# Attention in front of two feed-forward layers: transposing probabilities by halves of the queries

## The chip, the cores and the metric

The kernel runs on one core of one Trainium2 chip. The metric is the device time of one execution in microseconds (us). The core has a matmul engine (TensorE, PE in the profile; its weight loads are shown apart as PEld), VectorE (DVE), ScalarE (ACT), GpSimd (POOL) and SyncE (SP), which issues most transfers. Each engine works through its own queue in order, and semaphores tie the queues together. TensorE writes only to PSUM, an accumulation memory of eight banks, from which DVE and ACT copy results out.

## The reference

Attention over two batches of eight heads, 768 positions, head size 64, each query seeing the last 128 positions and the first four ("sinks"), and two feed-forward layers of width 512 to 2048 to 512 on the 1536 tokens:

```python
keep = is_sink | in_window
scores = np.where(keep, scale * np.matmul(q, k.transpose(0, 1, 3, 2)), -1000000000.0)
a = np.exp(scores - np.max(scores, axis=-1, keepdims=True))
a = a / (np.sum(a, axis=-1, keepdims=True) + 1e-09)
x = np.matmul(a, v).transpose(0, 2, 1, 3).reshape(B * S, H * D)
h = np.maximum(x @ w_in, 0.0)
x = h * h @ w_out
h = x @ moe2_w_in
out = (h * np.tanh(softplus(h))) @ moe2_w_out
```

## The kernel before

The program has two stages. The first, up to about 106 us, is attention; the second is the two layers, whose matmuls (L620 and L636) fill the rest of the span.

Attention goes by blocks of 128 queries, 12 in all (tile number t), each with the 128 positions before it, its own 128 and a strip of 16 sink columns: at most 272 columns of scores. Heads are taken two at a time; a block has four such *pairs* (j = 0 to 3), and there are 48 pairs. The loop at L541 walks over *slots* n, one per pair; in each slot several pairs are at different steps. `at[d]` is the pair n + d, and `last` holds the d whose pair is the last of its block. The order in which the code emits work is the order of every engine's queue.

- `emit_s` (L350): scores of a pair on PE. Six matmuls, three for each of the two heads; queries and keys are split into a high and a low part (`qh`, `ql`, `kh`, `kl`). Each matmul has 64 rows (the head size), and the two heads lie in the upper and the lower 64 rows of the array.
- `emit_max` (L363): adds the mask and takes the maximum, on DVE, once per head.
- `emit_exp` (L372): the exponential and its sum, on ACT, once per head, into `pr`.
- `emit_rs` (L384): adds up the sums and takes their reciprocal for two pairs, on DVE. `emit_norm` (L395): multiplies the probabilities of a pair by it, on POOL.
- `emit_t` (L401): transposes the probabilities of a pair on PE, 128x128 each, against the identity; two heads and up to two blocks of keys make four. They go into one PSUM bank (`pt`). `evac_t` (L411) copies the bank to `pts`, on DVE where j is 0 (`EV = (0,)`, L181) and on ACT otherwise.
- `emit_av` (L420): the products with v, with `pts` as the moving operand; each fills 64 of the array's 128 columns.
- `emit_sink` (L435, POOL), `emit_sink_t` (L443, PE), `evac_sink` (L452, DVE) and `emit_sink_mm` (L458, PE): gathers, transposes, copies and multiplies the sink columns of a whole block.
- `emit_x` and `split_x` (L474, L480): the finished block out of its one PSUM bank, high part on ACT (`xh`), low part on DVE (`xl`).
- `prep` (L294) and `place_prep` (L317): transposes q or k of a later block on PE (L302, four of 128x128), copies the high part on ACT (L314), subtracts for the low part on DVE (L320).

The steady state has a rhythm of two slots. In an even slot PE has the scores of pair n + 4, `prep`, the transposes of pairs n - 1 and n, and behind the last pair of a block its sink transpose. In an odd slot it has scores and the products with v of pairs n - 3 and n - 2, and the sink products. The scores have four PSUM banks, two pairs' worth; `pt` and the transposes of q and k share three; the products with v have one. Four blocks of the first layer's weights are converted on the side (L129 to L166) in some of the slots.

Of the kernel before, what the change touches and what calls it, by code (L numbers as in the profile page):

```python
# [9 lines left out]
F32 = mybir.dt.float32  # L10
# [7 lines left out]
P = 128  # L18
# [10 lines left out]
def kernel(  # L29
# [13 lines left out]
    nc = tc.nc  # L43
    B, H, S, D = q.shape
# [4 lines left out]
    NPAIR = H // 2  # L49
# [131 lines left out]
    EV = (0,)  # L181
# [146 lines left out]
    def geom(i):  # L328

        if i == 0:  # L330
            return kpos(0), P, mask0, None, 0, None
        if i == 1:
            return kpos(0), 2 * P, mask1, 0, P, None
        if i % 2 == 0:
            return kpos(i - 1), WIN, mask_e, 0, P + SK, P
        return kpos(i - 1) - SK, WIN, mask_o, SK, SK + P, 0
# [5 lines left out]
    pair_no = {p: m for m, p in enumerate(pairs)}  # L342

    def sum_at(b, i, j):
        g, s = divmod(pair_no[b, i, j] + 1, 2)
        return sums[g % len(sums)], s
    st = {}
    pr = {}
# [49 lines left out]
        x = pr[b, i][:, 2 * j : 2 * j + 2, 0:w]  # L398
        nc.gpsimd.tensor_tensor(out=x, in0=x, in1=rs.to_broadcast([P, 2, w]), op=ALU.mult)  # L399

    def emit_t(b, i, j):  # L401
        _, _, _, op, oc, _ = geom(i)
        pt = ps_p.tile([P, 2, 2, P], F32, tag="pt", name="pt")
        for e in range(2):
            h = 2 * j + e
            if op is not None:
                nc.tensor.transpose(pt[:, 0, e, :], pr[b, i][:, h, op : op + P], ident)  # L407
            nc.tensor.transpose(pt[:, 1, e, :], pr[b, i][:, h, oc : oc + P], ident)  # L408
        st["pt", b, i, j] = pt

    def evac_t(b, i, j):  # L411
        pt = st.pop(("pt", b, i, j))
        pts = apool.tile([P, 2, 2, P], F32, tag="pts", name="pts", bufs=3)
        c = slice(0 if i else 1, 2)
        (nc.vector.tensor_copy if j in EV else nc.scalar.copy)(pts[:, c], pt[:, c])
        st["pts", b, i, j] = pts

    av = {}

    def emit_av(b, i, j):  # L420
        _, _, _, op, _, os_ = geom(i)
        if j == 0:
            av[b, i] = ps_a.tile([P, NPAIR, P], F32, tag="av", name="av")
        pts = st.pop(("pts", b, i, j))
        blocks = [(1, i)] if op is None else [(0, i - 1), (1, i)]
        for m, (c, kb) in enumerate(blocks):
            for e in range(2):
                nc.tensor.matmul(  # L428
                    av[b, i][e * D : (e + 1) * D, j, :], lhsT=vn[b, kb][:, 2 * j + e, :],
                    rhs=pts[:, c, e, :], start=(j == 0 and m == 0),  # L430
                    stop=(j == NPAIR - 1 and m == len(blocks) - 1 and os_ is None),
                    skip_group_check=True,
                )
# [60 lines left out]
    with tc.manual_schedule():  # L494
        load_limits()
        nc.scalar.preload_act_table_set("natural_log_exp_and_others")
        load_tile(0, "qk", halves=2)
        load_tile(1, "qk")
        load_tile(2, "kq")
        load_tile(0, "v")  # L500
        load_tile(3, "kq")
        positions()
        load_tile(1, "v")
        load_vsink(0)
        load_tile(2, "v")
        load_tile(3, "v")
        warm = apool.tile([P, P], F32, name="warm")
        nc.vector.memset(warm, 0.0)
        nc.vector.memset(one, 1.0)
        nc.gpsimd.memset(two, 2.0)  # L510
        for x in sums:
            nc.vector.memset(x, 1e-9)
        idle = ps_a.tile([P, P + 2], F32, tag="av", name="idle")

        def keep_warm(times):
            for _ in range(times):
                nc.tensor.matmul(idle[:, 0:P], lhsT=warm, rhs=warm, start=True, stop=True)  # L517

        keep_warm(WARM[0])
        limits(idle[:, P : P + 2])  # L520
        first_mask()
        prep(0, "q", 0)
        place_prep()
        keep_warm(WARM[1])
        prep(0, "k", 0)
        place_prep()
        keep_warm(WARM[2])
        emit_s(*pairs[0])
        emit_max(*pairs[0], 0)
        emit_max(*pairs[0], 1)  # L530
        prep(0, "q", 1)
        place_prep()
        prep(0, "k", 1)
        place_prep()
        emit_s(*pairs[1])
        emit_max(*pairs[1], 0)
        emit_max(*pairs[1], 1)
        second_mask()
        window_masks()
        emit_exp(*pairs[0])  # L540
        for n in range(-3, NPR + 4):  # L541
            at = {d: pairs[n + d] for d in range(-3, 5) if 0 <= n + d < NPR}
            last = {d for d in at if at[d][2] == NPAIR - 1}
            t, j = divmod(n, NPAIR)
            if 4 in at and n > -3:
                emit_s(*at[4])
            if 3 in at and n > -3:
                emit_exp(*at[3])
            if n % 2 == 0:
                group = [at[d] for d in (1, 2) if d in at]  # L550
                if group:
                    emit_rs(group)
                for p in group:
                    emit_norm(*p)
                    if p[2] == NPAIR - 1:
                        emit_sink(*p[:2])
            if -3 in last:
                emit_x(*at[-3][:2])
            if 4 in at and n > -3:
                emit_max(*at[4], 0)  # L560
                emit_max(*at[4], 1)
            split_x()


            if n % 2 == 0:
                if n >= 0:
                    prep(t + 2, "kq"[j // 2])
                for d in (-1, 0):
                    if d in at:
                        emit_t(*at[d])  # L570
                if -1 in last:
                    emit_sink_t(*at[-1][:2], st["s", *at[4]][0] if 4 in at else None)
            else:
                for d in (-3, -2):
                    if d in at:
                        emit_av(*at[d])
                if -2 in last:
                    emit_sink_mm(*at[-2][:2])
            if -1 in at:
                evac_t(*at[-1])  # L580
            if n in (-3, -2):
                prep(1, "qk"[n + 3])
            place_prep()
            evac_sink()
            if n >= 0 and j == NPAIR - 1:
                load_tile(t + 4, "q")
                load_tile(t + 4, "k")
                load_tile(t + 4, "v")
            if n == -1 or (n >= 0 and t < len(tiles) - 1 and (t % NB, j) == (NB - 1, 2)):
                sink_keys()  # L590
            if n < 0:
                keep_warm(WARM[3])
            if n == 1:
                fast_flag()
                load_vsink(1)
            if n in (5, 13):
                spread_vsink(n // 8)
            for m, x in enumerate(blocks):
                step = CONV_STEPS.get(n - CONV_AT[0] - CONV_AT[1] * m)
                if step:  # L600
                    getattr(x, step)()
# [416 lines left out]
```

## Time and profile before

| | |
|---|---|
| median of 3 runs | 636.59 us (635.65 to 636.65) |
| span of the profiled execution | 633.9 us |
| total of the profiled execution | not listed; the median of the runs lies 2.7 us over the span |
| PE busy | 623.8 us, 98% of the span |
| DVE, ACT, POOL busy | 461.6, 364.1, 71.1 us |
| attention stage | the first 106 us |

The span runs from the first to the last instruction of one profiled execution. A busy PE is not a PE at its peak, as matmuls are pipelined and one's end overlaps the next one's start. So the rows below go by starts: from the start of one group of instructions to the start of the next.

### The profile page before, as it was taken

Reading aid. Unit: us, or ns where it says so; the run is one execution under the profiler, and the core shown is the slowest. Engines: PE = TensorE matmul, PEld = TensorE weight load, DVE = VectorE, ACT = ScalarE, POOL = GpSimd, SP = SyncE. Lnnn points to the kernel's source line nnn. Section 1 sums busy time; section 2 is a strip of 40 time slices with the busy share of each in tenths; the row PEclk is TensorE's granted clock in tenths of the full one; section 3 lists DMA queues with packets and bytes.
Section 4 is the critical chain, followed back from the end, with each engine's and each line's share of the span. In section 5 each row is a group of like instructions: output and inputs, shape, how many; then the busy total and the mean of one; then the engine's idle time right before and its main releaser. Section 6 shows DMA issues by size and latency. Waiting matters only on the chain.

```text
span 633.9 us, 9250 instructions
## 1 busy us (share of the span) xinstructions
PE 623.8 (98%) x3382; PEld 515.3 (81%) x3382; DVE 461.6 (73%) x967; ACT 364.1 (57%) x745; POOL 71.1 (11%) x97
## 2 busy tenths in 40 slices
PE   8999999999999999999999999999999999999995
PEld 7878877888888888888888888888888888888884
DVE  6988983999842111138988879999888888888883
ACT  5988985777744333347777655555454444454441
POOL 4786773000000000000000000000000000000000
PEclk9999999999999999999999999999999999999998
DMA  9644630666630000005566600000010000010001
GB/s 205 152 121 101 165 125 8 199 203 199 197 100 0 2 0 1 0 1 187 185 195 198 199 0 1 0 2 1 1 66 1 1 1 1 22 46 0 2 0 71
DMA packets 60968, 46.87 MB, mean 74 GB/s; under 512 B 38900, under 2 KB 55284, under 8 KB 60916
## 3 DMA queue, kind: packets, MB, share of 16 engines
q1 hardware_dynamic: 60768, 45.95, 24.5%
q8 instruction: 28, 0.46, 0.3%
q10 hardware_dynamic: 148, 0.26, 0.1%
q14 instruction: 24, 0.20, 0.1%
HBM read 43.06 MB, written 3.15 MB: 73 GB/s over the span
## 4 chain that ended last, share of the span: by engine, by line
PE 96%; DVE 2%; ACT 1%; issue 0%; DVEq 0%
PE h L620 41%; PE o L636 41%; PE s L356 4%; PE av L428 3%; PE tr L302 2%; PE pt L408 1%; PE pt L407 1%; PE idle L517 1%; PE av L464 1%; DVE s L367 1%; ACT pr L379 0%; DVE cv_a L147 0%; DVE cv_r L137 0%; ACT kh L314 0%; DVE cv_r L141 0%
## 5 line engine op out<-in xcount | busy, mean ns | idle before, releaser
L620 PE MATMUL h<-xl,wih 128*128 128x512 f32 x384 | 103.2, 390 | 0.0
L620 PE MATMUL h<-xh,wil 128*128 128x512 f32 x384 | 103.0, 390 | 0.0
L620 PE MATMUL h<-xh,wih 128*128 128x512 f32 x384 | 102.6, 389 | 0.0
L687 DVE TENSOR_TENSOR gl<-h,gh 128x512 fp32r<-128x512 f32 x48 | 33.2, 691 | 92.7 <-ACT gh L683 92.7
L620 PEld LDWEIGHTS h<-xl,wih 128*128 128x128 f32 x384 | 72.0, 188 | 15.2 <-issue 0.3
L620 PEld LDWEIGHTS h<-xh,wih 128*128 128x128 f32 x384 | 72.1, 188 | 15.0
L620 PEld LDWEIGHTS h<-xh,wil 128*128 128x128 f32 x384 | 71.9, 188 | 15.0 <-issue 0.2
L703 ACT ACTIVATE e<-t,small 128x512 f32<-128x512 f32 x48 | 34.8, 725 | 70.4 <-DVE t L699 70.4
L636 PE MATMUL o<-gh,wol 128*128 128x512 f32 x192 | 74.7, 389 | 0.0
L636 PE MATMUL o<-gl,woh 128*128 128x512 f32 x192 | 74.7, 389 | 0.0
L636 PE MATMUL o<-gh,woh 128*128 128x512 f32 x192 | 74.7, 389 | 0.0
L681 ACT ACTIVATE h<-h 128x512 f32<-128x512 f32 x48 | 27.9, 582 | 77.4 <-PE h L620 77.3
L636 PE MATMUL o<-wol,gh 128*128 128x512 f32 x176 | 68.5, 389 | 0.0
L636 PE MATMUL o<-woh,gl 128*128 128x512 f32 x176 | 68.5, 389 | 0.0
L636 PE MATMUL o<-woh,gh 128*128 128x512 f32 x176 | 68.5, 389 | 0.0
L719 ACT CAST gh<-t 128x512 fp32r<-128x512 f32 x44 | 27.4, 623 | 46.4 <-PE o L636 43.0
L399 POOL TENSOR_TENSOR pr<-pr,rs 128x544 f32<-128x544 f32 (+2 forms) x48 | 48.4, 1022 | 23.0 <-DVE rs L391 15.2
L147 DVE SCALAR_TENSOR_TENSOR cv_a<-cv_a,cv_r 128x512 int32<-128x512 int32 x64 | 44.5, 695 | 6.5 <-ACT h L681 0.5
L379 ACT ACTIVATE pr<-s,nm 128x272 f32<-128x272 f32 (+2 forms) x96 | 44.4, 477 | 5.1 <-DVE nm L367 2.6
L724 DVE TENSOR_TENSOR gl<-t,gh 128x512 fp32r<-128x512 f32 x44 | 30.3, 690 | 19.8 <-ACT gh L719 19.8
L636 PEld LDWEIGHTS o<-gl,woh 128*128 128x128 f32 x192 | 36.1, 188 | 7.6
L636 PEld LDWEIGHTS o<-gh,wol 128*128 128x128 f32 x192 | 36.0, 188 | 7.5
(119 smaller groups left out, 1100.6 us busy)
## 6 DMA issues: line engine op xcount, KB each, us to landing
raw<-in_moe_w_in_dram SPq DMA_DIRECT2D x32, 512.0 KB, 3.9
raw<-in_moe_w_out_dram SPq DMA_DIRECT2D x32, 512.0 KB, 4.2
vn<-in_v_dram SPq DMA_DIRECT2D x12, 256.0 KB, 2.9
qn<-in_q_dram SPq DMA_DIRECT2D x11, 256.0 KB, 4.3
kn<-in_k_dram SPq DMA_DIRECT2D x11, 256.0 KB, 4.2
out_dram<-ob SPq DMA_DIRECT2D x4, 512.0 KB, 3.6
out_dram<-o SPq DMA_DIRECT2D x3, 256.0 KB
qn<-in_q_dram SPq DMA_DIRECT2D x2, 128.0 KB, 2.9
```

Source lines behind the costliest of these rows:

```text
L147: nc.vector.scalar_tensor_tensor(out=ai, in0=ai, scalar=3, in1=self.r, op0=ALU.logical_shift_left, op1=ALU.bitwise_or)
L356: nc.tensor.matmul(banks[e][:, 0:w], lhsT=x[b, i][r, j, :], rhs=y[r, j, c0 : c0 + w], start=(m == 0), stop=(m == 2),)
L379: nc.scalar.activation(out=pr[b, i][:, 2 * j + e, 0:w], in_=banks[e][:, 0:w], func=AF.Exp, bias=nm[:, e : e + 1], scale=-1.0, accum_out=sm ...
L399: nc.gpsimd.tensor_tensor(out=x, in0=x, in1=rs.to_broadcast([P, 2, w]), op=ALU.mult)
L428: nc.tensor.matmul(av[b, i][e * D : (e + 1) * D, j, :], lhsT=vn[b, kb][:, 2 * j + e, :], rhs=pts[:, c, e, :], start=(j == 0 and m == 0), s ...
L620: nc.tensor.matmul(ph, lhsT=w[a][:, d, :], rhs=x[:, d, :], start=(m == 0 and d == 0), stop=(m == 2 and d == NDC - 1),)
L636: nc.tensor.matmul(acc[sp][t], lhsT=a, rhs=x, start=(fb == 0 and m == 0), stop=(fb == NFB - 1 and m == 2),)
L681: nc.scalar.activation(out=ph, in_=ph, func=AF.Relu)
L687: nc.vector.tensor_tensor(out=gl, in0=hp.pop(n), in1=f32(gh), op=ALU.subtract)
L703: nc.scalar.activation(out=e, in_=t, func=AF.Ln, bias=two)
L719: nc.scalar.copy(g_tiles(n)[0], et[n][1])
L724: nc.vector.tensor_tensor(out=gl, in0=t, in1=f32(gh), op=ALU.subtract)
```

## The change

The transposes of the probabilities are cut by queries: the upper and the lower 64 rows (queries) of a block are transposed apart, each against a 64x64 corner of the identity, into one of two PSUM banks, so that 64 rows of the array take part in each. Two pairs are transposed together, and each of the two banks holds one half of the queries of both pairs. Each bank is copied out in a slot of its own, into alternate runs of 64 columns of `pts`.

The order in the slots changes with it. Transposes of q and k and the sink transpose move from even slots to odd ones, ahead of the products with v. The transposes of an even slot are those of pairs n and n + 1 in place of n - 1 and n; sums and normalisation are those of n + 2 and n + 3 in place of n + 1 and n + 2, and they are emitted behind the maxima of pair n + 4.

```diff
     def sum_at(b, i, j):
-        g, s = divmod(pair_no[b, i, j] + 1, 2)
+        g, s = divmod(pair_no[b, i, j], 2)
...
+    def emit_t(group):
+        banks = [ps_p.tile([P, 2, 2, 2, P // 2], F32, tag="pt", name="pt") for _ in range(2)]
+        for s, (b, i, j) in enumerate(group):
+            _, _, _, op, oc, _ = geom(i)
+            for e in range(2):
+                for c, o in enumerate((op, oc)):
+                    if o is None:
+                        continue
+                    for r in range(2):
+                        rows = slice(r * D, (r + 1) * D)
+                        nc.tensor.transpose(
+                            banks[r][:, s, c, e, :], pr[b, i][rows, 2 * j + e, o : o + P], ident[rows, rows]
+                        )
+        pts = apool.tile([P, 2, 2, 2, P], F32, tag="pts", name="pts", bufs=2)
+        for s, p in enumerate(group):
+            st["pts", p] = pts[:, s]
+        st["evac"] = [(group, banks[r], pts[..., r * D : (r + 1) * D], r) for r in range(2)]
+
+    def evac_t(eng=None):
+        if not st.get("evac"):
+            return
+        group, x, y, r = st["evac"].pop(0)
+        copy = nc.vector.tensor_copy if r and pair_no[group[0]] % 4 in EV else nc.scalar.copy
+        c0 = [0 if i else 1 for _, i, _ in group]
+        if len(set(c0)) == 1:
+            copy(y[:, : len(group), c0[0] :], x[:, : len(group), c0[0] :])
+        else:
+            for s, c in enumerate(c0):
+                copy(y[:, s, c:], x[:, s, c:])
...
+            if -3 in last:
+                emit_x(*at[-3][:2])
+            if 4 in at and n > -3:
+                emit_max(*at[4], 0)
+                emit_max(*at[4], 1)
             if n % 2 == 0:
-                group = [at[d] for d in (1, 2) if d in at]
+                group = [at[d] for d in (2, 3) if d in at]
                 if group:
                     emit_rs(group)
                 for p in group:
                     emit_norm(*p)
                     if p[2] == NPAIR - 1:
                         emit_sink(*p[:2])
-            if -3 in last:
-                emit_x(*at[-3][:2])
-            if 4 in at and n > -3:
-                emit_max(*at[4], 0)
-                emit_max(*at[4], 1)
             split_x()
             if n % 2 == 0:
-                if n >= 0:
-                    prep(t + 2, "kq"[j // 2])
-                for d in (-1, 0):
-                    if d in at:
-                        emit_t(*at[d])
-                if -1 in last:
-                    emit_sink_t(*at[-1][:2], st["s", *at[4]][0] if 4 in at else None)
+                if 0 in at:
+                    emit_t([at[0], at[1]])
             else:
+                if n >= -1:
+                    prep(*((t + 3, "k") if j == NPAIR - 1 else (t + 2, "q")))
+                if 0 in last:
+                    emit_sink_t(*at[0][:2], st["s", *at[4]][0] if 4 in at else None)
                 for d in (-3, -2):
                     if d in at:
                         emit_av(*at[d])
                 if -2 in last:
                     emit_sink_mm(*at[-2][:2])
-            if -1 in at:
-                evac_t(*at[-1])
+            evac_t()
```

## Rows read from the trace of the kernel before

**Rows 1.** The page: the chain that ended last, shares by engine.
```profile
PE 96%; DVE 2%; ACT 1%; issue 0%; DVEq 0%
```
**Rows 2.** Windows of 10 us: PE, PEld, DVE, ACT, POOL busy (instructions); granted clock.
```profile
20.00:30.00 10.00, 10.00 (x109) 8.26 (x110) 9.23 (x37) 9.77 (x33) 7.09 (x8) 1.00 0.39 103
...
sum 70.00, PE 68.92 PEld 57.14 DVE 62.31 ACT 62.59 POOL 51.41; mean PE 9.85 PEld 8.16 DVE 8.90 ACT 8.94 POOL 7.34
```
**Rows 3.** Weight loads in order of time, 70 to 74 us: start, us, what.
```profile
70.14 0.19 PEld L356 LDWEIGHTS s<-kh,qh 64*128 64x128 f32 x2 [0.17 <-ACT qh L314]
...
70.71 0.85 PEld L428 LDWEIGHTS av<-pts,vn 128*64 128x64 f32 x16
71.74 0.19 PEld L356 LDWEIGHTS s<-kh,qh 64*128 64x128 f32 x2 [0.17 <-issue]
71.84 0.19 PEld L356 LDWEIGHTS s<-kh,ql 64*128 64x128 f32 x2
71.97 0.19 PEld L356 LDWEIGHTS s<-kl,qh 64*128 64x128 f32 x2
72.31 0.42 PEld L302 LDWEIGHTS tr<-ident,kn 128*128 128x128 f32 x4
72.70 0.14 PEld L407 LDWEIGHTS pt<-ident,pr 128*128 128x128 f32 x1
...
73.46 0.14 PEld L408 LDWEIGHTS pt<-ident,pr 128*128 128x128 f32 x1
73.77 0.19 PEld L356 LDWEIGHTS s<-kh,qh 64*128 64x128 f32 x2 [0.17 <-ACT pr L379]
```
**Rows 4.** Weight loads from 92.2 us, a group of transposes with no tr ahead.
```profile
92.87 0.14 PEld L407 LDWEIGHTS pt<-ident,pr 128*128 128x128 f32 x1
92.93 0.14 PEld L408 LDWEIGHTS pt<-ident,pr 128*128 128x128 f32 x1
```
**Rows 5.** The chain that ended last, in order of time: start us, us, what.
```profile
83.47 0.87 PE av L464 x16
```
**Rows 6.** Groups of ACT's instructions, 20 to 90 us: count, busy us, mean ns.
```profile
L415 ACT COPY pts<-pt 128x512 f32<-128x512 f32 x24 | 14.5, 602 | 0.0
...
L314 ACT CAST kh<-tr 128x512 fp32r<-128x512 f32 x8 | 4.7, 586 | 1.2 <-PE tr L302 0.9
```
**Rows 7.** The page: transfers, count, KB each, median us to landing.
```profile
kn<-in_k_dram SPq DMA_DIRECT2D x11, 256.0 KB, 4.2
```
**Rows 8.** DVE in order of time from 73.4 us.
```profile
73.49 0.15 DVE L390 TENSOR_REDUCE rs<-sum 128x4 f32<-128x8 f32 x1
...
73.77 0.42 DVE L367 CUSTOM_DVE_ANT_0 s<-s,mask_o 128x272 f32<-128x272 f32 x1
...
74.51 0.69 DVE L320 TENSOR_TENSOR kl<-tr,kh 128x512 fp32r<-128x512 f32 x1
```
**Rows 9.** POOL in order of time from 73.4 us.
```profile
74.00 2.15 POOL L399 TENSOR_TENSOR pr<-pr,rs 128x544 f32<-128x544 f32 x2 [2.56 <-DVE rs L391]
```
**Rows 10.** Who waited for whom, 14 to 104 us: total us, times, longest.
```profile
PEld s L356 <- ACT pr L379: 2.5, 11, 0.6
...
PEld pt L407 <- POOL pr L399: 0.2, 1, 0.2
```
**Rows 11.** Groups of PE's instructions, 20 to 90 us.
```profile
L408 PE MATMUL pt<-ident,pr 128*128 128x128 f32 x72 | 16.0, 273 | 0.0
L407 PE MATMUL pt<-ident,pr 128*128 128x128 f32 x64 | 15.0, 274 | 0.0
```
**Rows 12.** Windows, 90 to 105.8 us, columns as in the earlier windows.
```profile
90.00:95.00 5.00, 4.60 (x60) 3.77 (x61) 5.00 (x17) 4.09 (x15) 3.89 (x5) 1.00 0.54 180
...
100.00:105.80 5.80, 5.80 (x66) 4.46 (x65) 0.98 (x2) 2.18 (x4) 0.70 (x2) 1.00 0.01 4
```
**Rows 13.** PE in order of time, 75 to 76.2 us, scores released apart.
```profile
75.69 0.51 PE L356 MATMUL s<-kh,ql 64*128 64x272 f32 x2
75.92 0.41 PE L356 MATMUL s<-kl,qh 64*128 64x272 f32 x2
```

More of the change, by code (lines that the diff above doesn't have):

```diff
@@ L399, in emit_norm @@
         nc.gpsimd.tensor_tensor(out=x, in0=x, in1=rs.to_broadcast([P, 2, w]), op=ALU.mult)
[L401 to L416, printed above, removed]
+    def emit_t(group):
[26 more added lines that the diff above has]
+                copy(y[:, s, c:], x[:, s, c:])
     av = {}
@@ L423, in emit_av @@
             av[b, i] = ps_a.tile([P, NPAIR, P], F32, tag="av", name="av")
-        pts = st.pop(("pts", b, i, j))
+        pts = st.pop(("pts", (b, i, j)))
         blocks = [(1, i)] if op is None else [(0, i - 1), (1, i)]
```

## The prediction

> **What bounds the kernel now.** I began with the page's chain of work that ended last: 96% of it lies on TensorE (PE) [rows 1]. Most of that is the two feed-forward layers, which the change doesn't touch; it touches the attention stage, up to about 106 us, so the question is what bounds that stage. The table of windows from 20 to 90 us answers only half: PE is busy 68.9 of 70 us, but VectorE (DVE) 62.3 and ScalarE (ACT) 62.6, or 89% each, and in its fullest window of 10 us ACT reaches 9.77 [rows 2]. The granted clock there is 1.00, so none of this is the clock. PE is first, two engines stand close behind it. A cheaper PE therefore can't shorten these 70 us by more than the distance to the second and third engine, and that distance is the main term of my sum.
>
> The timeline of PE's weight loads shows one steady period of two slots [rows 3]. A score group (L356) starts at 70.14, the products with v (L428) at 70.71, the next scores at 71.74, the transposes of keys (L302) at 72.31, those of the probabilities (L407/L408) at 72.70, the next scores at 73.77: 0.57 + 1.03 + 0.57 + 0.39 + 1.07 = 3.63 us. Inside a group the loads follow each other evenly: a pair of score matmuls (two heads, in the two row halves of the array) every 0.11 to 0.13 us, a transpose every 0.11 us. Between groups of a different layout there is more: 0.34 us from the last score pair to the first transpose, 0.31 us from the last transpose to the next scores. So a change of layout costs about 0.2 us, and the period has four (64x128 scores to 128x128 transposes, back, to 128x64 products, back). From tr to pt, both 128x128, there is none.
>
> **PE's part of the change.** (1) *Layouts.* The probabilities' transposes become 64x128, as the scores are, so in an even slot scores, transposes and the next scores share one layout; the transposes of q and k go to the odd slot between scores and products. The changes left are scores to tr, tr to av, av to scores: three in place of four, 0.2 us saved per period. No row shows 64x128 transposes beside 64x128 scores; the nearest, tr to pt, shows no gap within a layout, and I take none.
>
> (2) *The transposes.* Eight of 128x128, 8 x 0.11 = 0.87 us, become sixteen of 64x128 in eight pairs, one pair into two PSUM banks. What does a pair cost? Two things pace a transpose, loading 128 columns of weights and streaming the identity's columns. They come apart at the first one of a group that stands alone: the second load begins 0.06 us after the first, and only from then on every 0.11 us [rows 4]. So the load takes 0.06 and the streaming of 128 columns 0.11. A half streams 64 columns, 0.055 us, so the load sets the pace: 0.06 us a pair if the two halves run side by side, 8 x 0.06 = 0.47 us. That they do is what the score pairs show: two loads and two matmuls of 64 rows every 0.12 us [rows 3]. Bounds: 0.47 us for the group below; above, no overlap and a load as long as today's whole transpose, 16 x 0.11 = 1.75 us. I take 0.47, plus 0.05 before the next scores for their own first load. The period on PE becomes 0.36 + 0.47 + 0.05 + 0.57 + 0.59 + 1.03 = 3.07 us (0.59 is tr with its change of layout): 0.56 us less.
>
> The Trainium skill, page "TensorE: Matmul & The Clock Gate", section "LDWEIGHTS (loading the stationary operand)", puts a weight load at columns/1.2 ns however few rows it has. By it 128 columns take 107 ns, a pair of halves costs as much as a whole transpose, the group stays at 0.87 us, and only the layout change is saved; that is the second rival. The row with 0.06 us speaks against it, for this kind of load.
>
> (3) *Sinks.* The sink's transpose (L449) now follows tr in the odd slot, same layout, 0.11 us as before. Its products (L464) stay behind those with v [rows 5].
>
> **The other engines.** Their work is the same in amount. Evacuations: still two of 512 elements per two pairs, still a quarter on DVE; they now write runs of 64 of a wider tile. The nearest row for such writes: the copy into kh, runs of 128 of a wide tile, takes 586 ns, the one into contiguous pts 602 [rows 6]. I take no change; the lower end is the same, as no row shows a gain from shorter runs, and the upper one a tenth more for each of the 24 copies on ACT in these 70 us, 24 x 0.06 = 1.4 us. The loads of q, k and v are issued as before. k of block t+3 is now prepared at slot 4t+3 in place of 4t+4, which leaves four slots, two periods or 7.3 us, from issue; the page gives 4.2 us from issue to landing [rows 7], so I count nothing; if that cover were gone, the lost slot would cost up to half a period, 1.8 us, per block of queries.
>
> The *order* changes. Normalisation of a pair (POOL, L399) was emitted one or two slots behind its exponential; for the later pair of each two it is now in the same slot, and DVE's reduction and reciprocal (L390, L391) stand behind both maxima of that slot. They must wait for ACT's two exponentials, and behind them on DVE wait xl, the low half of q or k and the next maxima. The way from scores to transposes, from rows: scores some 0.45 us (of the 0.57 above), two maxima 0.74 (74.51 - 73.77), reduction and reciprocal 0.28 (73.77 - 73.49), then 0.2 to POOL, two normalisations 2.15 [rows 8, 9]: with 0.3 for the hand-overs 4.1 us from the start of the scores of an even slot to the second half of the next even slot's transposes. PE gets there after one period plus 0.6 us, 3.7 us in a period without sink products and 4.6 with the 0.87 us of L464. So in every second period some 0.1 to 0.4 us are missing even if DVE is never late. Between 14 and 104 us of the kernel before, PE waited for POOL once, 0.2 us [rows 10].
>
> **The sum.** From 20 to 90 us lie 136 whole transposes of probabilities [rows 11], 17 full groups, so PE alone would allow 17 x 0.56 = 9.5 us. DVE and ACT don't: 62.6 us of ACT work fit in no less. Between today's mean of 89% and the best window's 97.7% I take 95%: 62.6/0.95 = 65.9 us, **-4.1 us** (ends: 91%, -1.2; 97.7%, -5.9). From 90 to 95 us DVE is busy throughout; from there to 105.8, when no scores are left, DVE is mostly idle, ACT half, and PE is full, with the first products of the feed-forward layer between those of attention [rows 12]. There PE's work counts in full: the last five pairs have 20 transposes, which at 0.05 us less each give 1.0 us, and one group with two layout changes goes, 0.4, against two sink transposes that now stand alone, +0.4: **-1.0** (-0.4 to -1.6). Late normalisations and a second bank that comes free after the first: **+0.7** (the 0.1 to 0.4 us above in the half of 17 periods without sink products give 0.9 to 3.4 us; other waits on PE hide part, so the ends are 0 and 3, and I take a value near the low one). Start-up, where inputs are awaited: 0. Together -4.4 us. The feed-forward stage follows on a full PE, so the gain reaches the end. The profiled execution has a span of 633.9 us; its own total is not listed, and the three runs have a median of 636.59, so 2.7 us lie around the span, which I carry unchanged: 629.5 us of span, **632.2 us**; this case by itself 629 to 635.3.
>
> **Rivals.** *First, the gain is swallowed (about 636.3, within 0.2%).* ACT and DVE are each idle 11%, but in pieces that the hand-overs need; scores already wait for ACT's exponentials in 11 places [rows 10], and PE with less to do only waits longer. For it: 97.7% in one window already [rows 2]. Against: PE's idle time is the smaller, 1.1 us of 70.
>
> *Second, the weight load sets the pace at 0.11 us a pair.* Then only layouts are saved, 0.2 x 24 = 4.8 us on PE, of which late normalisations take about half: about 634. For it: the even 0.11 us of all transposes. Against: 0.06 behind the first.
>
> *Third, on the other side: normalisation becomes the bound (about 639.5).* Each even slot's transposes wait for POOL by what is missing above, 0.1 to 0.4 us, plus whatever DVE or ACT run late. The change saves 0.56 us a period, so from a lateness of about 0.3 us on the wait takes more than it gives. Price at 0.45 us late: 0.25 + 0.45 - 0.56 = 0.14 us in some 20 periods of the stage, +2.8 us. A wait that releases the two halves of a pair apart adds to it: score pairs released apart run at 0.2 us and more a pair in place of 0.12 [rows 13]. For it: the reduction in the rows began 1.2 us after its scores had ended. Against: a waiting PE lets DVE and ACT catch up.
>
> **Numbers.** Forecast 0.50, swallowed 0.17, weight load 0.18, normalisation 0.15. A difference of 0.2%, 1.27 us, is about what a measurement of this kernel can tell from none. Faster, in the order of the cases: 0.47 + 0.05 + 0.16 + 0 = 0.68; same: 0.02 + 0.10 + 0.01 + 0.03 = 0.16; slower: 0.01 + 0.02 + 0.01 + 0.12 = 0.16. The range goes a little past the forecast's best end, for evacuations and waits of which no row tells, and takes in most of the third rival: 628.3 to 638.8.
>
> **What would show it.** Right: half transposes in pairs every 0.06 us and no 0.2 us gap beside them; a period near 3.4 us, 3.9 and more with sink products; ACT and DVE at 95% between 20 us and the last scores; PE with idle time put down to ACT and POOL. Wrong: pairs at 0.11 us or halves one after the other; gaps within the even slot; PE's weight loads of pt waiting for POOL by over 0.5 us in most periods; DVE idle before L390 for ACT; evacuations well over 0.6 us.

## The result, and the profile after

The changed kernel takes 640.63 us (median of 6 runs, 639.3 to 642.31) against 635.87 us for the kernel before (635.31 to 636.65): 1.0073 times, interval 1.0063 to 1.0083. It is slower by 4.8 us, where 4.4 us of gain were forecast.

The page of the changed kernel, its busy times and its chain:

```profile
PE 618.4 (97%) x3558; PEld 511.3 (80%) x3558; DVE 463.3 (73%) x965; ACT 364.3 (57%) x745; POOL 71.5 (11%) x97
...
PE 90%; DVE 5%; ACT 1%; issue 1%; POOL 1%; POOLq 0%; ACTq 0%
```

PE is busy 5.4 us less over the span (623.8 before); its work fell by more, since a lower clock stretched part of it (last section). The chain that ended last lies on it by 90% in place of 96% [rows 1]; DVE went from 2% to 5%. The windows of the changed kernel from 20 to 90 us, the sum, and then the window from 90 to 100 us of the kernel before and of the changed kernel:

```profile
sum 70.00, PE 61.94 PEld 50.84 DVE 59.22 ACT 59.41 POOL 50.08; mean PE 8.85 PEld 7.26 DVE 8.46 ACT 8.49 POOL 7.15
...
90.00:100.00 10.00, 9.60 (x119) 7.72 (x120) 6.92 (x26) 6.73 (x23) 8.69 (x9) 1.00 0.31 103
...
90.00:100.00 10.00, 6.51 (x106) 5.55 (x106) 9.83 (x33) 8.25 (x27) 6.21 (x6) 1.00 0.36 107
```

The first line answers to [rows 2]. PE fell from 68.92 to 61.94 us, as it was meant to. But DVE and ACT, which were to rise from 89 to 95%, fell to 85%. Every engine has more time off, so the stage is held up by hand-overs between engines, no longer by the work of one. The last blocks suffer most for their length: from 90 to 100 us PE is idle 3.5 us, where it was 0.4. The weight loads of one period in order of time:

```profile
28.74 0.19 PEld L356 LDWEIGHTS s<-kh,qh 64*128 64x128 f32 x2 [0.17 <-issue]
...
28.98 0.19 PEld L356 LDWEIGHTS s<-kl,qh 64*128 64x128 f32 x2
29.11 0.64 PEld L411 LDWEIGHTS pt<-ident,pr 64*128 64x128 f32 x16
29.66 0.20 PEld L356 LDWEIGHTS s<-kh,qh 64*128 64x128 f32 x2
...
29.91 0.19 PEld L356 LDWEIGHTS s<-kl,qh 64*128 64x128 f32 x2
30.25 0.42 PEld L302 LDWEIGHTS tr<-ident,kn 128*128 128x128 f32 x4
31.67 0.14 PEld L462 LDWEIGHTS s<-ident,psg 128*128 128x128 f32 x1 [1.00 <-issue]
31.93 0.85 PEld L441 LDWEIGHTS av<-pts,vn 128*64 128x64 f32 x16
32.95 0.18 PEld L356 LDWEIGHTS s<-kh,qh 64*128 64x128 f32 x2 [0.17 <-issue]
```

Set this beside [rows 3]. From the last scores to the first half transpose it is 0.13 us, as inside a group, where the change of layout took 0.34. Sixteen halves take 0.55 us to the next scores, which follow without a gap. The period lasts 4.21 us. From the start of the transposes of keys (30.25) to the sink transpose there are 1.42 us, where four transposes take 0.39 [rows 3]; without that stop of 1.03 us the period would be 3.18 us, and the forecast was 3.07 plus 0.11 for the sink transpose. The stop is the news. In the same stretch the rows of DVE, POOL and PE in order of time:

```profile
29.42 0.45 DVE L367 CUSTOM_DVE_ANT_0 s<-s,mask_o 128x272 f32<-128x272 f32 x1 [0.20 <-PE s L356]
...
30.18 0.16 DVE L390 TENSOR_REDUCE rs<-sum 128x4 f32<-128x8 f32 x1
...
30.48 0.66 DVE L496 TENSOR_TENSOR xl<-av,xh 128x512 fp32r<-128x512 f32 x1
30.73 2.15 POOL L399 TENSOR_TENSOR pr<-pr,rs 128x544 f32<-128x544 f32 x2 [1.01 <-DVE rs L391]
...
31.06 0.44 DVE L367 CUSTOM_DVE_ANT_0 s<-s,mask_o 128x272 f32<-128x272 f32 x1
...
31.70 0.30 PE L462 MATMUL s<-ident,psg 128*128 128x128 f32 x1 [0.80 <-DVE nm L367]
```

The sink transpose (L462) is written into spare columns of the first score bank of its slot's pair, n + 4. The scores of that pair ended at about 30.2 us; DVE took their maximum only from 31.06 on, because two maxima, the reduction and xl of the even slot stand ahead of it in DVE's queue, and PE stood still until that maximum had released the bank. Before the change, the eight transposes of probabilities lay between scores and sink transpose too, and by then the bank was free: PE waited there for a maximum once, 0.2 us. The waits of the changed kernel, 14 to 112 us (total us, times, longest; rows of PEld and of PE are two views of one engine, so like is to be compared with like):

```profile
POOL pr L399 <- ACT pr L379: 12.9, 6, 3.5
...
PEld s L462 <- issue: 8.2, 6, 2.0
PE s L462 <- DVE nm L367: 8.2, 7, 1.8
...
PEld s L356 <- ACT pr L379: 3.5, 12, 1.0
...
PEld pt L411 <- POOL pr L399: 2.4, 6, 0.7
...
PE av L441 <- DVE xl L496: 0.5, 2, 0.3
```

Two things are new beside [rows 10]: 8.2 us of PE's time in seven stops at the sink transpose, and 2.4 us in six waits for the normalisation on POOL, which had been one of 0.2 us. And POOL itself waits 12.9 us for ACT's exponentials, in six places, where it was 1.9 us in three.

### The profile page after: what moved, and what is told of

The parts are those of the page before. It is cut to its first block, busy times and chain, and to the rows that moved or that the text cites. A ratio compares the mean times of both kernels' runs of the same rounds, so it can differ in the third digit from the quotient of the medians.

```text
span 638.9 us, 9605 instructions
## 1 busy us (share of the span) xinstructions
PE 618.4 (97%) x3558; PEld 511.3 (80%) x3558; DVE 463.3 (73%) x965; ACT 364.3 (57%) x745; POOL 71.5 (11%) x97
## 4 chain that ended last, share of the span: by engine, by line
PE 90%; DVE 5%; ACT 1%; issue 1%; POOL 1%; POOLq 0%; ACTq 0%
PE h L631 41%; PE o L647 41%; PE av L441 3%; PE s L356 2%; DVE s L367 2%; PE tr L302 1%; ACT pr L379 1%; DVE xl L496 1%; PE pt L411 1%; PE idle L530 1%; PE av L477 1%; POOL pr L399 1%; DVE nm L367 1%; DVE cv_r L141 1%; DVE ql L320 0%
## 5 line engine op out<-in xcount | busy, mean ns | idle before, releaser
L647 PEld LDWEIGHTS o<-gh,woh 128*128 128x128 f32 x192 | 36.1, 188 | 7.5
```

The lines of the kernel that those rows point to most:

```text
L647: nc.tensor.matmul(acc[sp][t], lhsT=a, rhs=x, start=(fb == 0 and m == 0), stop=(fb == NFB - 1 and m == 2),)
```

## The experiments

The times below are medians; 'before' runs on the same chip gave 635.9 to 636.2 us, and the ratios are to these. Kernels of different series ran on different chips, so a few tenths of a us between two of them say little.

**First theory: the sink transpose's stop is the loss.** Four kernels. The first puts the sink transpose behind the products with v of its slot:

```diff
-                if 0 in last:
-                    emit_sink_t(*at[0][:2], st["s", *at[4]][0] if 4 in at else None)
                 for d in (-3, -2):
                     if d in at:
                         emit_av(*at[d])
+                if 0 in last:
+                    emit_sink_t(*at[0][:2], st["s", *at[4]][0] if 4 in at else None)
```

> The changed kernel with the sink transpose (L462) moved behind the products with v of the same odd slot. Theory 1: the changed kernel is slow because the sink transpose, now right behind the transposes of q or k, is written into a score bank that DVE's maximum still holds, and PE stands still for it 7 times, 8.2 us in all. Then these waits go, seven layout changes of 0.2 us come, and the time is 632 to 635 us, below the kernel before. Theory 2 (the prediction's third rival): normalisation is late and sets the end; the sink's wait only hides it. Then PE waits for POOL in the next slot instead, and the time stays at 639 to 641 us.

Measured: 640.04 us, 1.0062 (1.0048 to 1.0076). The second emits it behind the scores and ahead of the maxima, so that the maximum waits for it and not the other way round:

```diff
+            if n % 2 and 0 in last:
+                emit_sink_t(*at[0][:2], st["s", *at[4]][0] if 4 in at else None)
             if 4 in at and n > -3:
                 emit_max(*at[4], 0)
...
-                if 0 in last:
-                    emit_sink_t(*at[0][:2], st["s", *at[4]][0] if 4 in at else None)
```

> The changed kernel with the sink transpose put right behind the scores, and emitted ahead of the maxima of that slot, so that DVE waits for PE and PE waits for nobody. Theory 1: PE's 8.2 us of waits go with no layout change added, the maxima of eight slots start some 0.4 us later: 631 to 634.5 us. Theory 2: 639 to 641 us.

Measured: 638.79 us, 1.0037 (1.0023 to 1.0051). The third takes the other score bank:

```diff
-                    emit_sink_t(*at[0][:2], st["s", *at[4]][0] if 4 in at else None)
+                    emit_sink_t(*at[0][:2], st["s", *at[4]][0][::-1] if 4 in at else None)
```

> The changed kernel with the sink transpose written into the bank of the pair's second head, whose maximum comes 0.4 us after the first head's. Theory 1: each of the seven waits is 0.4 us longer: 643 to 644 us. Theory 2: no difference, 640 to 641 us.

Measured: 642.31 us, 1.0092 (1.0076 to 1.0107). The fourth takes the kernel before and moves the sink transpose alone:

```diff
                 if n >= 0:
                     prep(t + 2, "kq"[j // 2])
+                if -1 in last:
+                    emit_sink_t(*at[-1][:2], st["s", *at[4]][0] if 4 in at else None)
                 for d in (-1, 0):
                     if d in at:
                         emit_t(*at[d])
-                if -1 in last:
-                    emit_sink_t(*at[-1][:2], st["s", *at[4]][0] if 4 in at else None)
```

> The kernel before, with the sink transpose alone moved: ahead of the probabilities' transposes of its slot, right behind the transposes of q or k, so that it no longer has eight transposes (0.87 us) between itself and the scores. Theory 1: it waits for DVE's maximum as in the changed kernel, 0.5 to 1.2 us in six or seven places: 638.5 to 643 us. Theory 2: order inside the slot is worth nothing, 635.5 to 636.5 us.

Measured: 637.67 us, 1.0023 (1.0014 to 1.0032). So the stop is real. With the later bank its seven places grew from 8.2 to 9.6 us and the time by 1.7 us, though the intervals of the two ratios overlap and the mean granted clock fell as well (0.989 to 0.994 in that kernel's executions, 0.991 to 0.998 in those of the changed kernel). The kernel before loses 1.6 us to the move; its trace has one stop there, of 1.1 us, where six or seven were expected. But taking the stop away from the changed kernel gave back 0.6 and 1.8 us of 4.8, not 6 to 9, and the 0.6 are no more than the clock: four of the five executions with the late sink transpose had 0.997 or 0.998 and took 639.6 to 640.5 us, the one of the changed kernel with 0.998 took 639.3. The first theory, that the stop alone is the loss, falls. Where the time went, the waits of the kernel with the late sink transpose:

```profile
PEld s L356 <- ACT pr L379: 5.5, 19, 1.0
...
PE av L441 <- DVE xl L496: 5.0, 8, 1.4
...
PEld pt L411 <- POOL pr L399: 4.3, 9, 0.8
```

Each of these grew: the products with v wait for xl 5.0 us in place of 0.5, the halves for POOL 4.3 in place of 2.4, scores for ACT 5.5 in place of 3.5. The sink's stop had stood in front of other waits.

**What are those waits?** Four kernels on top of the second one above (638.79 us, the base from here on). Whole transposes again, in the changed order, one pair to a bank and a bank copied out per slot:

```diff
...
-                    for r in range(2):
-                        rows = slice(r * D, (r + 1) * D)
-                        nc.tensor.transpose(
-                            banks[r][:, s, c, e, :], pr[b, i][rows, 2 * j + e, o : o + P], ident[rows, rows]
-                        )
+                    nc.tensor.transpose(banks[s][:, c, e, :], pr[b, i][:, 2 * j + e, o : o + P], ident)
...
```

> The kernel of e2_sink_ahead (changed order, sink transpose ahead of the maxima) with whole transposes of 128x128 again, one pair per bank. PE gets 0.41 us of transposes and two layout changes of 0.2 us more per period. If PE's work set the pace, 20 periods would cost 16 us: about 655 us. If PE idles by 0.5 to 1 us a period for other engines, as the waits of the changed kernel say, most of it is taken up: 640 to 645 us.

Measured: 639.17 us, 1.0051 (1.0036 to 1.0067). PE is busy 68.43 of 70 us again, and the time is that of the halves within 0.4 us. What the halves save on PE is, in this order, nearly all waited away. Part of this is again the clock, which falls behind long waits of PE (last section): the halves' only execution at 0.998 took 637.94 us, 1.2 us less than whole transposes, all of whose executions had 0.997 or 0.998. Next, the transposes of q and k go back to the even slot, ahead of the halves in one kernel (this diff) and behind `emit_t` in the other:

```diff
             if n % 2 == 0:
+                if n >= 0:
+                    prep(t + 2, "kq"[j // 2])
                 if 0 in at:
                     emit_t([at[0], at[1]])
             else:
-                if n >= -1:
-                    prep(*((t + 3, "k") if j == NPAIR - 1 else (t + 2, "q")))
```

> The kernel of e2_sink_ahead with the transposes of q and k back in the even slot, between scores and halves, as before the change: one layout change more, 0.2 us a period on PE, but scores of successive slots are again 1.7 and 1.9 us apart in place of 0.9 and 2.2, and the halves come 0.6 us later behind their normalisation. Theory 3 (scores come in bunches, DVE and ACT stand still between them, and only two pairs of score banks bridge it): 633 to 636 us. Theory 2 (late normalisation): also a gain, 635 to 637. Theory 4 (the low half of the finished block, xl, stands behind reduction and maxima on DVE, and the products with v wait for it): no gain, 638 to 639 us.

Measured: 635.05 us, 0.9985 (0.9976 to 0.9994).

> As e6, but with the transposes of q and k behind the halves in the even slot: scores are as evenly spaced as in e6, while the halves come as early behind their normalisation as in the changed kernel. Theory 3: 633 to 637 us, near e6. Theory 2: no gain over e2, 638 to 640 us. Theory 4: 638 to 640 us.

Measured: 639.59 us, 1.0055 (1.0041 to 1.0069). In both, the scores are equally spaced, so the bunching of scores (theory 3) isn't it: it would have helped both. The two differ in the order of two groups in one slot and by 4.5 us. My reading was that ahead of the halves, the transposes of q and k are 0.6 us of work that PE has to do anyway while it would wait for normalised probabilities, and that behind them they cover nothing. The traces bear out half of it. The halves' waits for POOL fell from 3.9 us in 11 places (the base) to 1.4 in 5 with the transposes ahead, but with the transposes behind they fell as much, to 1.3 in 3. What that second kernel has instead is ACT waiting for the late transposes of q and k:

```profile
ACT qh L314 <- PE tr L302: 6.1, 9, 1.5
...
ACT kh L314 <- PE tr L302: 3.8, 8, 0.7
```

These are 9.9 us in 17 places, and 1.5 us in 4 with the transposes ahead. So the place of these transposes is worth 3.7 us by the times; whether by what they cover or by what waits for them isn't shown. The fourth leaves the normalisation out:

```diff
-        nc.gpsimd.tensor_tensor(out=x, in0=x, in1=rs.to_broadcast([P, 2, w]), op=ALU.mult)
+        if (b, i, j) == pairs[-1]:
+            nc.gpsimd.tensor_tensor(out=x, in0=x, in1=rs.to_broadcast([P, 2, w]), op=ALU.mult)
```

> The kernel of e2_sink_ahead without the normalisation on POOL (left out for all pairs but the last, so the output is that of undivided exponentials); reductions and reciprocals stay on DVE. Theory 2: transposes no longer wait for POOL, and the time falls to 631 to 634 us. Theories 3 and 4: the wait moves to the next hand-over, 636.5 to 638.5 us.

Measured: 631.75 us, 0.9936 (0.9921 to 0.9952), 7.0 us less than the base. Its control makes the same edit in the kernel before:

> The control to e8: the kernel before without the normalisation on POOL (left out for all pairs but the last, so the output is that of undivided exponentials). Theory 2: in the kernel before normalisation was in time and PE was full, so the time hardly falls: 634.5 to 636 us, against 7 us in the changed order. If POOL's work slows the other engines as such, whatever its lateness: 629 to 632 us here too.

Measured: 634.09 us, 0.9973 (0.9964 to 0.9983), 2.1 us less than before. A little of the 7.0 us is thus there in either order, which I hadn't expected; 4.9 us are there in the changed order alone. That these are all lateness isn't shown: leaving POOL's work out also ends a slowdown of DVE that comes with it (last section), and that is worse in the changed order.

**Can normalisation be in time?** The reduction is parted, so that the earlier pair, whose exponential is a slot old, is reduced and normalised ahead of the maxima:

```diff
+            if n % 2 == 0 and 2 in at:
+                emit_rs([at[2]])
+                emit_norm(*at[2])
             if -3 in last:
                 emit_x(*at[-3][:2])
...
             if 4 in at and n > -3:
                 emit_max(*at[4], 0)
                 emit_max(*at[4], 1)
-            if n % 2 == 0:
-                group = [at[d] for d in (2, 3) if d in at]
...
+            if n % 2 == 0 and 3 in at:
+                emit_rs([at[3]])
+                emit_norm(*at[3])
...
```

> The kernel of e2_sink_ahead with the reduction of two pairs parted: the earlier pair, whose exponential is one slot old, is reduced and normalised ahead of the slot's maxima, the later one behind them as in the changed kernel. 0.28 us more on DVE per period. Theory 2 in the form 'the reduction stands behind two maxima and an exponential of its own slot, so POOL begins late': POOL starts about 0.8 us sooner and the second pair is ready by as much as the first normalisation no longer waits: 634 to 637 us, against 638.8 of e2. If POOL's 2.2 us of work in a row, not its start, were late: 638.5 to 640 us.

Measured: 636.39 us, 1.0009 (0.9999 to 1.0018): 2.4 us off the base. Its waits:

```profile
PEld s L356 <- ACT pr L379: 5.6, 19, 0.6
...
PE av L441 <- DVE xl L496: 5.4, 8, 1.3
```

Of the halves' waits for POOL one is left, 0.3 us (the base had 3.9 us in 11). Those for ACT and for xl stay. The opposite, in the kernel before: reduction and normalisation behind the maxima, with their old pairs.

```diff
-            if n % 2 == 0:
-                group = [at[d] for d in (1, 2) if d in at]
...
             if 4 in at and n > -3:
                 emit_max(*at[4], 0)
                 emit_max(*at[4], 1)
+            if n % 2 == 0:
+                group = [at[d] for d in (1, 2) if d in at]
...
```

> The kernel before with one thing changed: reduction and normalisation emitted behind the maxima of their slot, with the old pairs, whose exponentials are a slot old. Theory 2: POOL starts some 0.8 us later and PE begins to wait for it now and then, since 0.8 us of slack were left: 636.5 to 638.5 us. If only the exponential of the same slot made normalisation late: 635.5 to 636.3 us.

Measured: 639.07 us, 1.0050 (1.0037 to 1.0063). This one move, with no transpose touched, costs the kernel before 3.1 us. Its waits show that this isn't only PE waiting for POOL:

```profile
PEld s L356 <- ACT pr L379: 3.4, 13, 0.6
...
PEld pt L407 <- POOL pr L399: 0.5, 1, 0.5
...
PE av L428 <- DVE xl L483: 2.5, 2, 1.5
```

Against 0.2, 2.5 and 1.4 us before, the wait for POOL grew by 0.3, that for ACT by 0.9, that for xl by 1.1. I expected POOL's to carry most of it; it doesn't. Part of the way from the late reduction to these waits is in DVE's own work. In two lines (L137, L141) it converts weights for the first layer, in slots that neither the change nor this move alters. These instructions in the kernel before, in this one, and in the kernel before without normalisation, 14 to 112 us (count, busy us, mean ns):

```profile
L137 DVE TENSOR_SCALAR cv_r<-raw 128x512 int32<-128x512 int32 x6 | 3.4, 566 | 0.0
L141 DVE TENSOR_SCALAR cv_r<-raw 128x512 uint16<-128x512 uint32 x6 | 3.1, 519 | 0.2
...
L137 DVE TENSOR_SCALAR cv_r<-raw 128x512 int32<-128x512 int32 x5 | 4.5, 892 | 0.0
L141 DVE TENSOR_SCALAR cv_r<-raw 128x512 uint16<-128x512 uint32 x5 | 4.5, 891 | 0.1
...
L141 DVE TENSOR_SCALAR cv_r<-raw 128x512 uint16<-128x512 uint32 x7 | 3.3, 466 | 0.2
L137 DVE TENSOR_SCALAR cv_r<-raw 128x512 int32<-128x512 int32 x7 | 2.9, 420 | 0.0
```

Normalisation that starts later falls upon them, and they take up to 1.24 us, about 3.5 us more for five pairs of them than in the kernel before. The longest wait for xl shows the way: one of them takes 1.05 us from 94.15 us, beside POOL's normalisation from 92.24 to 94.88; the maxima, the reduction and xl (96.97) stand behind it on DVE, and PE waits 1.5 us for xl, until 97.78. That this makes up the whole 3.1 us isn't shown.

Then halves with the distances of the kernel before: slots are swapped, so that odd slots have `emit_rs` (pairs n + 1 and n + 2, ahead of the maxima), the transposes of q and k, the halves (pairs n - 1 and n) and behind them the sink transpose; the products with v come a slot later.

```diff
-            if n % 2 == 0:
-                group = [at[d] for d in (2, 3) if d in at]
+            if n % 2:
+                group = [at[d] for d in (1, 2) if d in at]
...
-                for d in (-3, -2):
...
+                for d in (-4, -3):
...
```

> Halves with the distances of the kernel before: transposes in odd slots so that the two pairs of a group are normalised two slots ahead and exponentiated at least one slot ahead of their reduction, reduction ahead of the maxima, transposes of q and k ahead of the halves; the products with v come one slot later. PE saves 0.41 us of transposes a period against the kernel before. Theory 2: with the lag restored the halves give what the prediction's sum gave, less a slot at the ends of the stage: 631.5 to 634.5 us. If ACT and DVE, 89% busy in the kernel before, leave nothing to gain: 635 to 637 us.

Measured: 636.64 us, 1.0013 (1.0003 to 1.0022). No gain. It has no waits for POOL among its longer ones, but scores wait 7.4 us in 26 places for ACT. That ACT and DVE left nothing can't be the reason: they are busy 61.63 and 61.02 of the 70 us from 20 to 90, less than in the kernel before. What it is stays open, as the later products with v changed with it. Last, the measures that helped, together (parted reduction, transposes of q and k ahead of the halves, sink transpose ahead of the maxima):

> The kernel of e6_tr_before_pt with the reduction parted as in e9. If lateness of the normalisation is what e6 still suffers from: 632.5 to 634.5 us, against 635.05 of e6. If e6 is bound by DVE and ACT themselves, the 0.28 us of DVE more per period cost: 635 to 637 us.

Measured: **632.80 us, 0.9949 (0.9936 to 0.9962)**, the fastest kernel here that still normalises, 3.2 us under the kernel before. With whole transposes instead, by the edit shown for whole transposes above:

> The kernel of e12_tr_split with whole transposes, one pair per bank: the same four layout changes, 0.41 us more of PE per period. If the halves are worth what they save on PE once normalisation is in time: 634.5 to 637 us, against 632.8 of e12. If all of e12's gain is its order: 632.5 to 633.5 us.

Measured: 635.28 us, 0.9990 (0.9981 to 1.0000). So the halves are worth 2.5 us once normalisation is in time, and 0.4 us, within the spread of the runs, where it is late (1.2 by the one execution at a like clock). The windows from 20 to 90 us of the fastest kernel:

```profile
sum 70.00, PE 66.57 PEld 53.31 DVE 65.85 ACT 64.29 POOL 52.70; mean PE 66.57 PEld 53.31 DVE 65.85 ACT 64.29 POOL 52.70
```

DVE is busy 94% and ACT 92%, near the 95% on which the forecast was built. DVE's share flatters, though: the parted reduction is twice as many instructions, 11.6 us of DVE's work in these windows, where the kernel with the same order and one reduction for two pairs has 5.9.

**The measures one by one on the changed kernel as it is**, with its sink transpose in place. The parted reduction alone, by its diff above:

> The changed kernel with the parted reduction of e9 alone, its sink transpose left where the change put it. Theory 2: most of what e9 gained over e2, 2.4 us, shows here too: 637.5 to 639 us. If the sink transpose's wait stands in the way while it is there: 640 to 641 us.

Measured: 639.71 us, 1.0058 (1.0042 to 1.0073). And the transposes of q and k alone, back ahead of the halves by the diff above:

> The changed kernel with the transposes of q and k back between scores and halves, its sink transpose left in the odd slot, now right behind the scores and so waiting longer for the maximum. Theory 2: the cover of 0.6 us ahead of the halves is worth some 3 us as in e6: 636 to 638 us. If the sink's wait takes it back: 639.5 to 641.5 us.

Measured: 645.03 us, 1.0144 (1.0126 to 1.0163), worse by 4.4 us where the same move on the base gained 3.7. The waits of that kernel:

```profile
PEld s L462 <- POOL pr L399: 8.5, 5, 2.4
...
PE s L462 <- DVE nm L367: 8.2, 6, 2.2
```

The sink transpose, now right behind the scores, stops PE for 9.9 us in seven places (one of them put down to POOL) and takes the whole gain back and more. Each of these two kernels has a twin above that differs in the place of the sink transpose alone: 639.71 and 636.39 us with the parted reduction, 645.03 and 635.05 us with the transposes of q and k moved, 640.63 and 638.79 us with neither. So the same move of the sink transpose is worth 3.3, 10.0 and 1.8 us, in part by the clock, which was 0.990 to 0.996 in the two kernels with the stop and 0.995 to 0.999 without. The parts of the loss don't add up one by one: the sink's stop hides the other waits, and each measure shows its worth only when the stop is gone.

## Why the prediction was wrong, point by point

- *What bounds the kernel*: right for the kernel before, PE first, DVE and ACT close behind; the fastest kernel has them 94 and 92% busy, DVE with added work. The changed kernel is bound by none of them.
- *Layouts*: right. 0.13 us in place of 0.34 from scores to halves, none behind them.
- *The transposes*: right in size. I took 0.47 + 0.05 us for sixteen halves; it is 0.55. A pair every 0.07 us decides against the second rival, which had 0.11. The Trainium skill, page "TensorE: Matmul & The Clock Gate", section "LDWEIGHTS (loading the stationary operand)", puts a load of 128 columns at 107 ns, by which eight pairs would take an estimated 0.86 us; the trace differs for these loads, and the trace decides.
- *Sinks: "now follows tr in the odd slot, same layout, 0.11 us as before"*. This step failed first. I counted the instruction and its layout, and not the bank that it writes. The row after: seven stops, 8.2 us. What the eight transposes before it had covered I had not asked.
- *The order: late normalisations, +0.7 us.* The mechanism and its place were right (the way from scores over maxima, reduction and POOL to the halves), the size was not: up to 4.9 us by the two kernels without normalisation, which take DVE's slowdown beside POOL out as well. I computed the way with DVE and ACT in time and put the shortfall of 0.1 to 0.4 us into the sum; that the reduction also waits for exponentials of its own slot, and that DVE and ACT run behind PE, I named in words and put into a rival, not into the sum.
- *The sum: ACT and DVE at 95%, -4.1 us.* This step failed too, because it let the busiest engine fill up and took the waits as a small correction. In the changed kernel they are busy 85%, and the time follows the waits. The windows 20 to 90 us of the kernel before say how much work there is, not whether a new order can pack it. The term for the tail, -1.0 us, failed the same way: it took PE as full behind 95 us, and PE is idle 3.1 us more than before from 90 to 100 us. The clock, 1.00 before and so left out, has a price now (last section). And the stated upper end of 635.3 us isn't the sum of the terms' own upper ends (-1.2, -0.4 and +3), which gives 638.0.
- *The third rival, normalisation becomes the bound, about 639.5 us, chance 0.15*: nearest to what was measured, 640.63. That nearness is luck. It priced a wait for POOL in some 20 periods, and its sign, over 0.5 us in most periods, did not come: the halves waited for POOL in six places, 2.4 us in all. The runs show that wait joined by the sink's stop, with the waits for xl and ACT behind both, and a lower clock. Its chance was too low for a change that moved a producer later and its consumer earlier, with 0.1 to 0.4 us missing on paper.
- *Swallowed gain*: wrong for the time, right for the halves in this order, which give next to nothing (639.17 us with whole transposes, 638.79 with halves).

What stays open: how much of the loss is lateness of the normalisation and how much its meeting DVE's conversion, which no run parted; by which way the place of the transposes of q and k is worth 3.7 us; and why the old distances with halves give no gain.

## What to carry to other kernels

When a step moves in an engine's order, ask what it covered for its neighbours, and who waits for its result: four transposes moved by one group were worth 3.7 us in all, and eight ahead of a write into a shared bank hid that bank's other user. A saving on the busiest engine is worth only what the hand-overs leave; the same halves gave 0.4 us in one order and 2.5 us in another. Taking the longest wait away shows what stands behind it; how much of its time comes back depends on the order around it, 1.8 us for 8.2 us of stops in one kernel here and 10.0 for 9.9 in another.

## What the runs showed of the hardware that I had not expected

**DVE beside POOL.** While POOL normalises, DVE's conversion instructions take longer. In the kernel before without normalisation, L141 has a mean of 0.47 us and L137 of 0.42 us (lines above); beside a normalisation on POOL, L141 took 1.05 to 1.35 us in every case but one in these traces, L137 anything from 0.40 to 1.30 us. DVE's work is thus not a fixed sum here: it depends on when POOL works. The chain of the changed kernel shows one case, in order of time, with POOL's normalisation running from 71.39 us:

```profile
71.66 1.13 DVE cv_r L137
...
72.81 1.24 DVE cv_r L141
...
75.58 0.64 PE s L356 x5
...
76.91 1.91 PE av L441 x16
...
82.41 1.02 PE av L441 x16
```

Behind the two conversions the chain runs over a maximum and ACT's exponential to the next scores, for which PE had stood still 0.87 us.

**The clock.** The granted clock of TensorE fell in the changed kernel. Windows of its trace (PE, PEld, DVE, ACT, POOL busy; then the granted clock):

```profile
73.00:76.00 3.00, 1.99 (x28) 1.51 (x28) 3.00 (x8) 1.66 (x6) 0.73 (x1) 1.00 0.03 5
76.00:80.00 4.00, 4.00 (x37) 3.25 (x36) 3.12 (x13) 2.96 (x11) 2.44 (x3) 0.57 0.06 15
97.00:100.00 3.00, 0.93 (x15) 0.74 (x15) 2.96 (x11) 2.36 (x8) 1.87 (x3) 1.00 0.35 134
100.00:104.00 4.00, 4.00 (x45) 3.43 (x47) 1.55 (x6) 2.01 (x6) 2.84 (x4) 0.57 0.00 0
```

After stretches in which PE was busy 1.99 of 3 us and 0.93 of 3 us, it ran for most of the next 4 us at half the clock, 1.2 in place of 2.4 GHz, though it was then busy throughout. Sixteen products with v took 1.91 us there and 1.02 us at the full clock (last two lines of the chain above). Eight us at a mean of 0.57 are an estimated 3.4 us of PE's time in the profiled execution. The kernel before had a clock of 1.00 in all windows of the stage [rows 2, 12]. So PE's stops cost a second time. How much of the 4.8 us this is, the six executions say roughly: the one with a mean clock of 0.998 took 639.30 us, the one with the lowest, 0.991, 642.31; the kernel before has 0.996 to 0.998. By the first of them the clock is an estimated 1.3 us of the median's 4.8, and the waits themselves are the rest.
